# Loading w_q and w_k together in wide rows, and projecting the first 256 tokens chunk by chunk over eight PSUM banks

## The chip, the cores and the metric

The kernel runs on one core of one Trainium2 chip. The metric is the device time of one execution in microseconds (us); lower is better. The engines are named as in the profile: PE (matmul), PEld (its weight loads), DVE, ACT, POOL, and SP, which here only issues DMAs.

## The reference

One transformer block on 2048 tokens of width 448: sliding-window attention (window 256, 16 heads of 28), then a gated MLP whose gate mixes tokens, both with adaptive layer norm. All in bf16.

```python
mod = (silu(c) @ w_mod).reshape(1, 6, 1, 448)        # c is (1, 448)
sa, ca, ga, sb, cb, gb = six rows of mod
h = layernorm(x) * (1 + ca) + sa
q, k, v = h @ wqkv, split into 16 heads of 28
p = softmax(q k^T * 28**-0.5, where 0 <= i - j < 256)
x = x + ga * ((p v) @ wo)
h = layernorm(x) * (1 + cb) + sb
z = gelu_tanh(h @ w_in);  z1, z2 = halves of 896;  z2 = layernorm(z2)
x = x + gb * ((z1 * (w_sp @ z2 + b_sp)) @ w_out)     # w_sp is (2048, 2048)
```

## The kernel before, in words

Tokens lie in 16 tiles of 128 (`x_sb`). The work is written as about 1200 operations, each made by `add` with the engines that may run it, its dependencies and the buffers or PSUM banks (`Hold`) that it takes. A string `ORDER` at the top of the file then says everything about the schedule: each word is `operation.engine`, followed by the number of the bank or buffer taken where there is one (`p` PE, `a` ACT, `v` DVE, `g` POOL, `s` SP). Every engine runs its words strictly in that sequence, SP's DMA issues too; `waits` puts in the semaphore waits that the dependencies need. So an instruction that waits holds everything behind it on its engine.

The start goes as follows. Token tiles 0 and 1 (`x_half` 0) are loaded first. ACT and SP load the first two sixths of `w_mod` (`d_wmAa`, `d_wmAb`, `d_wmAc`), SP then w_q and w_k into `wq_st`. All matrices of 448 rows are cut into contraction chunks kc = 0, 1, 2 (128 rows each) and 3 (64 rows), and loaded in three pieces: kc 2, kc 0 and 1, kc 3. Matmuls with a single column (L485) make the shift and scale `modT` out of `w_mod`. Meanwhile the layer-norm statistics of the tiles run on DVE (L549, L552, L554) with the power on POOL (L557), and the normalised `xn` (L569 on DVE, L573 on ACT) is transposed by PE (L627) two tiles and two chunks at a time; the evacuation `hT` (L634 ACT, L636 DVE) applies scale and shift. The weights are repacked from 28 to 32 columns a head by `pad` (L540 ACT or DVE, L541 POOL in the trace) into `WQK`.

The first 512 tokens are projected in two halves of 256 (`hf` 0 and 1), in eight groups of four heads: g = 0 to 3 are queries, 4 to 7 keys. For `hf` 0 the matmuls (L676) go chunk by chunk in the order kc = 2, 1, 0, 3 (`FIRST`), so that they can begin before all chunks are there; for `hf` 1 a group's four chunks go at once. In the kernel before, the loop runs over queries and keys in turn (`qk`): four groups' banks are held, the chunks of the first two are spread over two pairs of groups, and one chain of dependencies (`done_`) runs through both pairs. Evacuations to `qT` and `KT` are on ACT (L703) or DVE (L704). Matmuls with no use for the result (`warm`, L506) fill PE's time at the start.

Scores (L826) of the first unit need all queries of the first 512 tokens and the keys of the first 256. Exponentials of scores are on ACT (L859, L891), masks on DVE and POOL (L869, L906, L909), P V on PE (L935). The output of attention and the second layer norm's `xn2` are transposed by DMA (`turn`, L429, on SP's queue), which also transposes `w_sp` into `wspA` and `wspB`. Then come the MLP's matmuls: L1014 (z2), L1060 (z1), L1084 (token mixing, groups of 16 matmuls into one of eight banks, each followed by L1088 on DVE, which adds `bsp_bc`, and L1091 on POOL, which multiplies by z1), and L1103 (the output).

Of the kernel before, what the change touches and what calls it, by code (L numbers as in the profile page):

```python
# [4 lines left out]
ACT = mybir.ActivationFunctionType  # L5
# [208 lines left out]
def bass_adaLN_cond__sliding_block__mixer_gmlp__prompt_kernel(  # L214
# [70 lines left out]
    KT, kt_off, kt_bytes = alloc("KT", [128, 4, S], BF16)  # L285
# [12 lines left out]
    qT, _, qt_bytes = alloc("qT", [128, 4, S], BF16, at=wspA_off)  # L298
# [4 lines left out]
    wq_st, _, wq_bytes = alloc("wq_st", [128, DC, 2 * D], BF16, at=z2_off + wmod_bytes)  # L303
# [16 lines left out]
    ps = nc.alloc_psum_tensor("ps", [128, 8, 512], F32)  # L320
# [11 lines left out]
    bA = View(banks, [(6,), (7,), (0,), (1,), (2,), (3,), (4,), (5,)])  # L332
# [23 lines left out]
    def x_load(e, i):  # L356
        return e.dma_start(x_sb[:, 4 * i:4 * i + 4, :], x_d[:, 4 * i:4 * i + 4, :])

    def head(name, eng, t, d, first, n, cols, prio, land, deps=(), least=2.9):

        if n == 64:
            return load(name, eng, 0.1, lambda e: e.dma_start(t[0:64, 3, cols], d[384:448, cols]), deps, prio, land, least)
        return load(name, eng, 0.1, lambda e: e.dma_start(t[:, first:first + n, cols], d[128 * first:128 * (first + n), cols].rearrange("(c p) n -> p c n", p=128)), deps, prio, land, least)

    def x_half(eng, i, prio, land, least):
        return load("d_x0%d" % i, eng, 0.25, lambda e: e.dma_start(x_sb[:, 2 * i:2 * i + 2, :], x_d[:, 2 * i:2 * i + 2, :]), (), prio, land, least)

    t_x0 = [x_half("sp", 0, -98.99, 2.9, 2.9), x_half("sp", 1, -98.935, 7.7, 3.5)]
    t_x = [None]
    ALL = slice(None)  # L370
    LO, HI, BOTH = slice(0, D), slice(D, 2 * D), slice(0, 2 * D)
    t_c = load("d_c", "act", 0.01, lambda e: e.dma_start(c_row[:, 0:D], c[0:1, :]), prio=-98.98, land=1.6, least=1.5)
    t_wmA = [head("d_wmAa", "act", wmod, w_mod, 0, 2, BOTH, -98.97, 5.0, least=4.2), head("d_wmAb", "sp", wmod, w_mod, 2, 1, BOTH, -98.97, 4.1, least=3.4),
             head("d_wmAc", "sp", wmod, w_mod, 3, 64, BOTH, -98.96, 5.5, least=3.8)]
    t_wq = []
    for k, (n, cols, at) in enumerate((("q", LO, (5.8, 6.6, 6.8)), ("k", HI, (8.1, 8.9, 9.1)))):
        a, b, c_ = [head("d_w%s%s" % (n, p), "sp", wq_st, A_wqkv, first, rows, cols, -98.95 + 0.03 * k + 0.004 * i, at[i], (), 3.9)
                    for i, (p, first, rows) in enumerate((("b", 2, 1), ("a", 0, 2), ("c", 3, 64)))]
        t_wq.append([b, b, a, c_])

# [30 lines left out]
    def either(da, fa, dd, fd, deps=(), prio=0.0, take=()):  # L411
        return add({"act": (da, fa), "dve": (dd, fd)}, deps, prio, take)
# [20 lines left out]
    def pe(dur, fns, deps=(), prio=0.0, take=(), shape="full"):  # L433
        op = add({"pe": (dur, fns)}, deps, prio, take, lat=0.2 if shape == "rows32" else PEL)
        op.shape = shape
        return op
# [106 lines left out]
    t_wqk = [[pad(kc, k, -49.5 + 0.2 * k) for kc in range(DC)] for k in range(2)]  # L543
# [40 lines left out]
    QK_ready = {}  # L584
    V_ready = {}
    qkv_ops = {}
    K_ready = {}
# [5 lines left out]
    for tb in range(NB4):  # L593
        v = 40.0 * tb - 50.0
# [12 lines left out]
        ms = []  # L607
# [14 lines left out]
        evh = [[None] * DC, [None] * DC]  # L622
        for hf in range(2 if tb == 0 else 0):
            xl = [xs[2 * hf], xs[2 * hf + 1]]
            for cp, chs in enumerate(((2, 0), (1, 3))):
                h = Hold(bX)
# [4 lines left out]
                for k in range(2):  # L631
                    ch = chs[k]
                    ev = either(
                        0.57, lambda e, h=h, ch=ch, k=k, hf=hf: e.activation(hT[:, ch, hf * 256:(hf + 1) * 256], pst(h, k * 256, (k + 1) * 256), ACT.Identity,  # L634
                                                                            bias=modT[:, ch:ch + 1], scale=modT[:, 4 + ch:5 + ch]),
                        0.41, lambda e, h=h, ch=ch, k=k, hf=hf: e.tensor_scalar(hT[:, ch, hf * 256:(hf + 1) * 256], pst(h, k * 256, (k + 1) * 256),  # L636
                                                                               modT[:, 4 + ch:5 + ch], modT[:, ch:ch + 1], ALU.mult, ALU.add),
                        [m, t_modA] + one_bank, v + 0.5 * hf + cp * 0.1)
# [8 lines left out]
        for cp in range(2 if tb == 1 else 0):  # L647
            h = Hold(bX)
# [9 lines left out]
            for k in range(2):  # L658
                ch = 2 * cp + k
                ev = either(  # L660
                    0.77, lambda e, h=h, ch=ch, k=k, tb=tb: e.activation(hT[:, ch, tb * 512:(tb + 1) * 512], pst(h, k * 512, (k + 1) * 512), ACT.Identity,
                                                                        bias=modT[:, ch:ch + 1], scale=modT[:, 4 + ch:5 + ch]),
                    0.55, lambda e, h=h, ch=ch, k=k, tb=tb: e.tensor_scalar(hT[:, ch, tb * 512:(tb + 1) * 512], pst(h, k * 512, (k + 1) * 512),
                                                                           modT[:, 4 + ch:5 + ch], modT[:, ch:ch + 1], ALU.mult, ALU.add),
                    m + [t_modA] + evs[2 * cp:], v + cp * 0.1)
# [7 lines left out]
        FIRST = (2, 1, 0, 3)  # L673

        def part(g, kc, h, hf):
            return lambda e: e.matmul(ps[:, h.slot[0], 0:256], lhsT=WQK[:, kc, 4 * g:4 * g + 4, :].rearrange("p a b -> p (a b)"),  # L676
                                      rhs=hT[:, kc, hf * 256:(hf + 1) * 256], start=(kc == FIRST[0]), stop=(kc == FIRST[-1]))

        MMH = 256 / 2400.0 + 0.003
        for hf in range(2 if tb == 0 else 0):  # L680
            for qk in range(2):
                four = range(4 * qk, 4 * qk + 4)
                hq = {g: Hold(bA) for g in four}
                last = {}
                vv = v + 1 + 0.5 * hf + 0.2 * qk
                if hf == 0:
                    done_ = []
                    for kc in FIRST[:-1]:
                        for n in range(2):
                            pair = four[2 * n:2 * n + 2]  # L690
                            done_ = [pe(2 * MMH, [part(g, kc, hq[g], hf) for g in pair], [evh[hf][kc], t_wqk[qk][kc], done_], vv + kc * 0.01, [] if kc != FIRST[0] else [hq[g] for g in pair])]
                            ms += done_
                    for g in four:
                        last[g] = pe(MMH, [part(g, FIRST[-1], hq[g], hf)], [evh[hf], t_wqk[qk], done_], vv + 0.03 + 0.001 * g)
                else:
                    for g in four:
                        last[g] = pe(4 * MMH, [part(g, kc, hq[g], hf) for kc in FIRST], [evh[hf], t_wqk[qk]], vv + 0.001 * g, [hq[g]])
                for g in four:
                    h = hq[g]
                    ms.append(last[g])  # L700
                    to = (lambda g=g, hf=hf: qT[:, g, hf * 256:(hf + 1) * 256]) if g < 4 else (lambda g=g, hf=hf: KT[:, g - 4, hf * 256:(hf + 1) * 256])
                    ev = either(
                        0.39, lambda e, h=h, to=to: e.activation(to(), ps[:, h.slot[0], 0:256], ACT.Copy),  # L703
                        0.43, lambda e, h=h, to=to: e.tensor_copy(to(), ps[:, h.slot[0], 0:256]),  # L704
                        [last[g]], vv)
                    h.until.append(ev)
                    if g < 4:
                        QK_ready.setdefault((g, 0), []).append(ev)
                    else:
                        for i in (2 * hf, 2 * hf + 1):  # L710
                            K_ready[(g - 4, i)] = ev
        for k, g in enumerate(range(0 if tb == 0 else 4 if tb in FINE else 8)):
            h = Hold(bX)
# [5 lines left out]
            if g < 4:  # L719
                to = lambda g=g, tb=tb: qT[:, g, tb * 512:(tb + 1) * 512]  # L720
            else:
                to = lambda g=g, tb=tb: KT[:, g - 4, tb * 512:(tb + 1) * 512]
            ev = either(
                0.6, lambda e, h=h, to=to: e.activation(to(), ps[:, h.slot[0], :], ACT.Copy),
                0.68, lambda e, h=h, to=to: e.tensor_copy(to(), ps[:, h.slot[0], :]),
                [m], v + 1 + k * 0.1)
# [6 lines left out]
        for i in range(4):  # L733
            t = 4 * tb + i
            if tb in FINE:
                v = 10.0 * t - 20.0
                h = Hold(bX)
# [4 lines left out]
                ev = either(  # L742
                    0.6, lambda e, h=h, t=t: e.activation(KT[:, :, t * 128:(t + 1) * 128], ps[:, h.slot[0], :].rearrange("p (g n) -> p g n", g=4), ACT.Copy),
                    0.68, lambda e, h=h, t=t: e.tensor_copy(KT[:, :, t * 128:(t + 1) * 128], ps[:, h.slot[0], :].rearrange("p (g n) -> p g n", g=4)),
                    [m], v + 1)
# [442 lines left out]
```

## Time and profile before

| | |
|---|---|
| device time, median of 3 runs | 271.91 us (271.07 to 272.81) |
| the profiled execution | 273.37 us, of which the profile's span is 271.5 us |
| PE busy | 260.9 us (96%), 2897 matmuls |
| PEld busy | 136.2 us (50%) |
| DVE busy | 155.2 us (57%) |
| ACT busy | 131.8 us (49%), nothing after 60% of the span |
| POOL busy | 133.1 us (49%) |
| HBM | 9.53 MB read, 1.84 MB written |

In the profile every line of an answer names a line of the kernel, an engine, an operation and its tiles, with how often it ran (x) and how long. In answers over stretches of time, the first number after the stretch is its length, followed by the busy time and count of each engine, the granted clock of PE (1.00 is full), the share of time that the DMA engines were busy and the GB/s that they moved. The time between an instruction's end and the next one's start is idle time, and the name after an arrow is what ended it. For a DMA the profile gives when it was issued, and the time from there to its landing.

### The profile page before, as it was taken

The page shows a single profiled execution, that of the slowest core. Times are in us where ns is not written, and L with a number is a line of the kernel's source. Part 1 is how long each engine was busy: PE and PEld are TensorE (multiplying, and loading weights), DVE is VectorE, ACT ScalarE, POOL GpSimd, SP SyncE. Part 2 cuts the span into 40 slices and gives each one's busy share as a digit, 9 for nine tenths or more (in the row PEclk, how much of TensorE's full clock was granted, in tenths as well). Part 3 has the DMA queues.
Part 4 walks back from the last instruction along what each step waited for, and adds up shares of the span by engine and source line. Part 5 has one row for each costly group of instructions (what it writes and reads, how often), then busy time and mean ns, then how long its engine had stood idle before and what let it go on. Part 6 is the DMA issues. An engine that isn't in the chain of part 4 may idle for free.

```text
span 271.5 us, 6828 instructions
## 1 busy us (share of the span) xinstructions
PE 260.9 (96%) x2897; PEld 136.2 (50%) x2916; DVE 155.2 (57%) x363; ACT 131.8 (49%) x190; POOL 133.1 (49%) x175
## 2 busy tenths in 40 slices
PE   7899999999999988999999999999999999999996
PEld 2674465556567555444444444444444444445454
DVE  6689998999999998973874000112233201314354
ACT  3589998999999993889896500000000000000000
POOL 5538756557279983856578000043477501633110
PEclk9799999999999999999999999999999999999999
DMA  7991668765273695838999990000000000000222
GB/s 214 269 334 38 141 109 106 136 99 128 56 119 64 114 94 92 205 77 102 191 176 221 170 197 16 0 2 0 0 0 2 0 0 0 2 17 17 85 69 86
DMA packets 66777, 25.45 MB, mean 94 GB/s; under 512 B 57846, under 2 KB 66043, under 8 KB 66747
## 3 DMA queue, kind: packets, MB, share of 16 engines
q1 hardware_dynamic: 66328, 24.52, 47.4%
q8 instruction: 23, 0.38, 0.6%
q10 hardware_dynamic: 418, 0.50, 0.6%
q14 instruction: 8, 0.06, 0.1%
HBM read 9.53 MB, written 1.84 MB: 42 GB/s over the span
## 4 chain that ended last, share of the span: by engine, by line
PE 81%; ACT 7%; DVE 5%; DMA 4%; issue 1%; ACTq 0%; DVEq 0%
PE ps L1084 35%; PE ps L1060 8%; PE ps L1103 8%; PE ps L1014 7%; PE ps L714 6%; PE ps L826 4%; ACT PA L859 4%; PE ps L935 3%; ACT PA L891 3%; PE ps L751 3%; PE ps L676 2%; DMA wmod<-in_w_mod_dram 2%; PE ps L958 2%; DMA hT<-o_sb 2%; DVE PA L906 1%
## 5 line engine op out<-in xcount | busy, mean ns | idle before, releaser
L1091 POOL TENSOR_TENSOR z1T<-tmpg,z1T 128x512 bf16<-128x512 bf16 x28 | 31.9, 1154 | 78.0 <-DVE tmpg L1088 78.0
L1088 DVE TENSOR_TENSOR tmpg<-ps,bsp_bc 128x512 bf16<-128x512 f32 x28 | 19.0, 690 | 81.7 <-PE ps L1084 70.6
L859 ACT ACTIVATE PA<-ps 128x1536 bf16<-128x1536 f32 (+4 forms) x64 | 60.3, 976 | 1.8 <-PE ps L826 1.0
L1084 PE MATMUL ps<-wspA,z 128*128 128x512 bf16 x220 | 49.1, 379 | 0.3 <-issue 0.2
L1084 PE MATMUL ps<-wspB,z 128*128 128x512 bf16 x218 | 49.0, 379 | 0.3
L1084 PEld LDWEIGHTS ps<-wspA,z 128*128 128x128 bf16 x224 | 21.9, 98 | 26.5 <-issue 0.4
L1084 PEld LDWEIGHTS ps<-wspB,z 128*128 128x128 bf16 x224 | 21.9, 98 | 26.4
L557 POOL TENSOR_TENSOR rs_all<-ve_all,neghalf 128x1 f32<-128x1 f32 (+1 forms) x31 | 21.2, 693 | 12.4 <-DVE ve_all L554 10.4
L869 POOL TENSOR_TENSOR PA<-PA,mask 128x1024 bf16<-128x1024 bf16 (+1 forms) x9 | 18.6, 2068 | 11.7 <-ACT PA L859 11.7
L935 PEld LDWEIGHTS ps<-Vaug,PA 128*128 128x128 bf16 x720 | 20.8, 96 | 4.8 <-issue 0.8
L1014 PE MATMUL ps<-w_in,hT 64*128 64x448 bf16 x224 | 22.4, 349 | 0.5 <-DVE PA L906 0.3
L935 PE MATMUL ps<-Vaug,PA 128*128 128x32 bf16 x720 | 22.1, 176 | 0.1
L1103 PE MATMUL ps<-w_out_g,z1T 128*128 128x448 bf16 (+3 forms) x126 | 21.9, 332 | 0.0
L1060 PE MATMUL ps<-hT,w_in 64*128 64x512 bf16 x196 | 21.8, 376 | 0.0
L826 PE MATMUL ps<-qT,KT 32*64 32x64 bf16 (+3 forms) x768 | 18.1, 223 | 2.1 <-ACT PA L859 1.0
L549 DVE BATCH_NORM_STATS2 st_all<-x_sb 128x6 f32<-128x448 bf16 x32 | 19.3, 612 | 0.1
L714 PE MATMUL ps<-hT,WQK 128*128 128x512 bf16 x72 | 17.9, 379 | 0.9 <-issue 0.3
L891 ACT ACTIVATE PA<-ps 128x1536 bf16<-128x1536 f32 (+1 forms) x16 | 16.4, 1024 | 1.6 <-PE ps L826 1.0
L906 DVE TENSOR_TENSOR PA<-PA,mask 128x2048 bf16<-128x2048 bf16 x14 | 17.0, 1212 | 0.2 <-ACT PA L859 0.2
L1114 DVE TENSOR_TENSOR fin<-ps,x_sb 128x448 bf16<-128x448 f32 (+3 forms) x18 | 10.0, 570 | 12.2 <-PE ps L1103 10.9
L1103 PEld LDWEIGHTS ps<-w_out_g,z1T 128*128 128x128 bf16 x126 | 11.8, 98 | 10.0 <-DVE fin L1114 0.2
L1068 ACT ACTIVATE z1T<-ps 128x512 bf16<-128x512 f32 x28 | 14.5, 608 | 3.6 <-PE ps L1060 3.5
(114 smaller groups left out, 334.8 us busy)
## 6 DMA issues: line engine op xcount, KB each, us to landing
w_in<-in_B_w_in_dram SPq DMA_DIRECT2D x8, 224.0 KB, 3.4
out_dram<-fin SPq DMA_DIRECT2D x15, 112.0 KB, 1.7
x_sb<-in_A_x_dram SPq DMA_DIRECT2D x3, 448.0 KB, 6.7
wmod<-in_w_mod_dram SPq DMA_DIRECT2D x1, 1344.0 KB, 10.3
w_out_g<-in_B_w_out_dram SPq DMA_DIRECT2D x1, 784.0 KB, 5.0
bsp_bc<-in_B_b_sp_dram SPq DMA_DIRECT2D x1, 512.0 KB, 4.6
x_sb<-in_A_x_dram SPq DMA_DIRECT2D x2, 224.0 KB, 4.0
wmod<-in_w_mod_dram SPq DMA_DIRECT2D x2, 224.0 KB, 5.6
```

The lines of the kernel that those rows point to most:

```text
L557: rs = pool(0.41 + 0.155 * len(tiles), lambda e: e.tensor_tensor(rs_all[:, slot, a:b], ve_all[:, slot, a:b], neghalf[:, 0:b - a], ALU.pow) ...
L714: m = pe(4 * MMS, [lambda e, h=h, g=g, kc=kc, tb=tb: e.matmul(ps[:, h.slot[0], :], lhsT=WQK[:, kc, 4 * g:4 * g + 4, :].rearrange("p a b -> ...
L826: return [lambda e, t=t: e.matmul(to(t), lhsT=KT[32 * t:32 * t + 32, qi, key:key + kn], rhs=qT[32 * t:32 * t + 32, qi, q0:q0 + qn], start= ...
L859: return e.activation(cols(place(kb, hf) + 64 + 768 * a, [[384, 2 * (b - a)], [1, w]]), ps[:, h.slot[0]:h.slot[0] + b - a, 2 * n * w:(2 * ...
L891: return e.activation(cols(EXTRAS[ext[n].slot[0]] + 128 * a, [[128, b - a], [512, 4], [1, 128]]), ps[:, h.slot[0]:h.slot[0] + b - a, :].re ...
L906: return e.tensor_tensor(cols(a, [[d, 2], [384, 16], [1, 64]]), cols(src(), [[0, 2], [64, 16], [1, 64]]), mask_ap([[64 if m else 192, 2], ...
L935: fns.append(lambda e, hO=hO, hd=hd, bi=bi, kb=kb, nb=nb, j=j, c=(2 * t + k) * 384 + 128 * (j - kb), half=half: e.matmul(ps[:, hO.slot[0], ...
L1014: return lambda e, kc, p0, start, stop: e.matmul(ps[:, hs[t % 2].slot[hf], 0:D], lhsT=hT[p0:p0 + 64, kc, t * 128:(t + 1) * 128], rhs=w_in[ ...
L1060: return lambda e, kc, p0, start, stop: e.matmul(ps[:, hs[b // 2].slot[b % 2], :], lhsT=w_in[p0:p0 + 64, kc, ft * 128:(ft + 1) * 128], rhs ...
L1084: m = pe(16 * MMS, [lambda e, h=h, si=si, ft=ft, tb=tb: e.matmul(ps[:, h.slot[0], :], lhsT=z2[:, si, ft * 128:(ft + 1) * 128], rhs=(wspA i ...
L1091: u = pool(1.16, lambda e, ht=ht, ft=ft, tb=tb: e.tensor_tensor(z1T[tb][:, ft, :], tmpg[:, ht.slot[0], :], z1T[tb][:, ft, :], ALU.mult), [ ...
L1103: return [lambda e, ft=ft: e.matmul(ps[:, h.slot[0], c0:c1], lhsT=z1T[t // 4][:, ft, (t % 4) * 128:(t % 4 + 1) * 128], rhs=w_out_g[:, ft, ...
```

## The change

The six loads of w_q and w_k (three pieces of each, rows of 448 elements) become three loads with rows of 896 elements, and the second pair of token tiles (`x_half` 1) is issued between the first and the second of them instead of between w_q and w_k. The projection of `hf` 0 holds eight banks, one for each group, and goes through its chunks for each pair of groups with a chain of dependencies of its own; `hf` 1's groups are made in one loop of eight.

```diff
-    t_x0 = [x_half("sp", 0, -98.99, 2.9, 2.9), x_half("sp", 1, -98.935, 7.7, 3.5)]
+    t_x0 = [x_half("sp", 0, -98.99, 2.9, 2.9), x_half("sp", 1, -98.94, 6.8, 3.5)]
...
-    t_wq = []
-    for k, (n, cols, at) in enumerate((("q", LO, (5.8, 6.6, 6.8)), ("k", HI, (8.1, 8.9, 9.1)))):
-        a, b, c_ = [head("d_w%s%s" % (n, p), "sp", wq_st, A_wqkv, first, rows, cols, -98.95 + 0.03 * k + 0.004 * i, at[i], (), 3.9)
-                    for i, (p, first, rows) in enumerate((("b", 2, 1), ("a", 0, 2), ("c", 3, 64)))]
-        t_wq.append([b, b, a, c_])
+    wqb, wqa, wqc = [head("d_wqk" + p, "sp", wq_st, A_wqkv, first, rows, BOTH, -98.95 + 0.02 * i, at, (), 3.9)
+                     for i, (p, first, rows, at) in enumerate((("b", 2, 1, 6.05), ("a", 0, 2, 7.9), ("c", 3, 64, 8.2)))]
+    t_wq = [[wqa, wqa, wqb, wqc]] * 2
...
         for hf in range(2 if tb == 0 else 0):
-            for qk in range(2):
-                four = range(4 * qk, 4 * qk + 4)
-                hq = {g: Hold(bA) for g in four}
-                last = {}
-                vv = v + 1 + 0.5 * hf + 0.2 * qk
+            hq = {g: Hold(bA) for g in range(8)}
+            last = {}
+            vv = v + 1 + 0.5 * hf
+            for n in range(4):
+                pair = (2 * n, 2 * n + 1)
+                done_ = []
                 if hf == 0:
-                    done_ = []
                     for kc in FIRST[:-1]:
-                        for n in range(2):
-                            pair = four[2 * n:2 * n + 2]
-                            done_ = [pe(2 * MMH, [part(g, kc, hq[g], hf) for g in pair], [evh[hf][kc], t_wqk[qk][kc], done_], ...)]
-                            ms += done_
-                    for g in four:
-                        last[g] = pe(MMH, [part(g, FIRST[-1], hq[g], hf)], [evh[hf], t_wqk[qk], done_], ...)
+                        done_ = [pe(2 * MMH, [part(g, kc, hq[g], hf) for g in pair], [evh[hf][kc], t_wqk[n // 2][kc], done_], ...)]
+                        ms += done_
+                for g in pair:
+                    if hf == 0:
+                        last[g] = pe(MMH, [part(g, FIRST[-1], hq[g], hf)], [evh[hf], t_wqk[n // 2], done_], ...)
+                    else:
+                        last[g] = pe(4 * MMH, [part(g, kc, hq[g], hf) for kc in FIRST], [evh[hf], t_wqk[n // 2]], ...)
```

The evacuations behind it are the same eight for each half. The whole `ORDER` string is another one. What it changes, read word by word against the one before:

- SP's first issues were: x pair 0, w_mod kc 2, w_mod kc 3, w_q kc 2, w_q kc 0 and 1, w_q kc 3, x pair 1, w_k kc 2, w_k kc 0 and 1, w_k kc 3, x tiles 4 to 7, w_v, w_mod (rest), w_v (last chunk), x tiles 8 to 11, and so on. They become: x pair 0, w_mod kc 2, w_mod kc 3, w_q and w_k kc 2, x pair 1, w_q and w_k kc 0 and 1, w_q and w_k kc 3, x tiles 4 to 7, w_o (last chunk), w_v (last chunk), x tiles 8 to 11, w_v, w_mod (rest), and so on. One transpose of `w_sp` that stood among the first 20 is moved behind the first transposes of attention. The load of `b_sp`, which had stood 12 `w_sp` transposes behind the last `hT` transpose, stands 24 behind it, and w_out is loaded behind that last `hT` transpose too.
- PE runs 16 `warm` matmuls instead of 13. The first transposes, the pairs of groups and the groups change places; when the first scores come, the same 32 matmuls of `hf` 0 and 20 of `hf` 1 stand before them.
- 86 of the operations go to another engine. At the start, the four evacuations of the first transposes are all on ACT (it was one), and the eight `pad` operations are three on DVE, three on POOL and two on ACT (they were five on ACT and three on POOL). DVE does the three of w_q's chunks 1, 0 and 3, among the statistics of token tiles 2 and 3.
- The activation L471, whose result nobody uses and which makes ACT load its table early, moves from the start of ACT's list to behind all but two of the MLP's activations.

More of the change, by code (lines that the diff above doesn't have):

```diff
@@ L688, in bass_adaLN_cond__sliding_block__mixer_gmlp__prompt_kernel @@
                     for kc in FIRST[:-1]:
-                        for n in range(2):
-                            pair = four[2 * n:2 * n + 2]
-                            done_ = [pe(2 * MMH, [part(g, kc, hq[g], hf) for g in pair], [evh[hf][kc], t_wqk[qk][kc], done_], vv + kc * 0.01, [] if kc != FIRST[0] else [hq[g] for g in pair])]
-                            ms += done_
-                    for g in four:
-                        last[g] = pe(MMH, [part(g, FIRST[-1], hq[g], hf)], [evh[hf], t_wqk[qk], done_], vv + 0.03 + 0.001 * g)
-                else:
-                    for g in four:
-                        last[g] = pe(4 * MMH, [part(g, kc, hq[g], hf) for kc in FIRST], [evh[hf], t_wqk[qk]], vv + 0.001 * g, [hq[g]])
@@ L698, in bass_adaLN_cond__sliding_block__mixer_gmlp__prompt_kernel @@
[L698 to L711, printed above, removed]
+                        done_ = [pe(2 * MMH, [part(g, kc, hq[g], hf) for g in pair], [evh[hf][kc], t_wqk[n // 2][kc], done_], vv + kc * 0.01, [] if kc != FIRST[0] else [hq[g] for g in pair])]
@@ new lines, in bass_adaLN_cond__sliding_block__mixer_gmlp__prompt_kernel @@
+                        ms += done_
+                for g in pair:
+                    if hf == 0:
+                        last[g] = pe(MMH, [part(g, FIRST[-1], hq[g], hf)], [evh[hf], t_wqk[n // 2], done_], vv + 0.03 + 0.001 * g)
+                    else:
+                        last[g] = pe(4 * MMH, [part(g, kc, hq[g], hf) for kc in FIRST], [evh[hf], t_wqk[n // 2]], vv + 0.001 * g, [hq[g]])
+            for g in range(8):
+                h = hq[g]
+                ms.append(last[g])
+                to = (lambda g=g, hf=hf: qT[:, g, hf * 256:(hf + 1) * 256]) if g < 4 else (lambda g=g, hf=hf: KT[:, g - 4, hf * 256:(hf + 1) * 256])
+                ev = either(
+                    0.39, lambda e, h=h, to=to: e.activation(to(), ps[:, h.slot[0], 0:256], ACT.Copy),
+                    0.43, lambda e, h=h, to=to: e.tensor_copy(to(), ps[:, h.slot[0], 0:256]),
+                    [last[g]], vv)
+                h.until.append(ev)
+                if g < 4:
+                    QK_ready.setdefault((g, 0), []).append(ev)
+                else:
+                    for i in (2 * hf, 2 * hf + 1):
+                        K_ready[(g - 4, i)] = ev
```

2 lines of the change are left out of this document (1 added, 1 removed).

## The prediction

> **What bounds the kernel now.** I read the engine shares first, then busy time by stretches, then the chain that ended last, then the first 20 us instruction by instruction.
>
> ```profile
> span 271.5 us, 6828 instructions
> ```
> ```profile
> 17.59:50.00 32.41, 31.14 (x553) 16.82 (x560) 30.07 (x68) 30.80 (x36) 22.96 (x21) 1.00 0.69 120
> 50.00:90.00 40.00, 38.86 (x902) 25.17 (x908) 38.45 (x80) 38.50 (x43) 25.05 (x32) 1.00 0.53 96
> 90.00:109.27 19.27, 17.45 (x368) 10.22 (x366) 18.18 (x42) 14.87 (x22) 13.92 (x18) 1.00 0.80 106
> 109.27:151.00 41.73, 41.59 (x400) 19.57 (x402) 27.45 (x89) 35.13 (x66) 27.45 (x52) 1.00 0.90 162
> 151.00:268.70 117.70, 117.21 (x564) 55.38 (x572) 28.01 (x44) 2.94 (x6) 34.81 (x31) 1.00 0.15 34
> ```
>
> The columns after the length are busy us of PE, PEld, DVE, ACT and POOL, then granted clock, DMA share and GB/s. From 109.27 us on PE is busy 99.6% of the time: no order of the same matmuls makes that part shorter. In the attention stage (17.59 to 90) PE, ACT and DVE are all about 95 to 97% busy. PE's gaps from 17.59 to 109.27 are 1.27 + 1.14 + 1.82 = 4.23 us; that is the most that a new order can win there, whatever it does. So the time is the moment at which the first scores (L826) start, plus a fixed amount of matmul work, plus these gaps.
>
> The start itself:
>
> ```profile
> 7.36 0.75 PE L485 MATMUL ps<-sc_sb,wmod 128*128 128x1 bf16 x24 [0.76 <-DMA wmod<-in_w_mod_dram]
> ```
> ```profile
> 9.69 3.61 PE L676 MATMUL ps<-hT,WQK 128*128 128x256 bf16 x22
> 13.54 0.61 PE L627 MATMUL ps<-ident,xn 128*128 128x128 bf16 x8 [0.24 <-ACT qT L703]
> 13.99 3.57 PE L676 MATMUL ps<-hT,WQK 128*128 128x256 bf16 x30
> 17.59 0.70 PE L826 MATMUL ps<-qT,KT 32*64 32x64 bf16 x64
> ```
> ```profile
> 9.86 0.62 DVE L549 BATCH_NORM_STATS2 st_all<-x_sb 128x6 f32<-128x448 bf16 x1
> ```
> ```profile
> 11.93 0.95 DVE L569 TENSOR_SCALAR xn<-x_sb,mv_all,rs_all 128x448 bf16<-128x448 bf16 x2
> ```
>
> The first 22 projection matmuls take 164 ns each, the next 30 take 119 ns: the clock.
>
> ```profile
> 8.00:8.25 0.25, 0.25 (x9) 0.19 (x5) 0.10 (x2) 0.25 (x1) 0.00 (x0) 1.00 1.12 380
> 8.50:8.75 0.25, 0.25 (x4) 0.25 (x5) 0.25 (x1) 0.06 (x2) 0.00 (x0) 0.50 0.56 179
> ```
> ```profile
> 12.00:12.25 0.25, 0.25 (x4) 0.23 (x3) 0.25 (x1) 0.00 (x0) 0.25 (x2) 1.00 1.03 143
> ```
>
> It is halved between about 8.4 and 11.8 us. When the first scores start, both versions have done the same matmuls (32 of the first 256 tokens, 20 of the next 256: four query groups and one key group), so that moment compares them fairly.
>
> **The change, part by part. The loads.**
>
> ```profile
> 2.41 1.05 SPq L363 DMA_DIRECT2D wq_st<-in_A_wqkv_dram  x2
> 3.51 0.48 SPq L362 DMA_DIRECT2D wq_st<-in_A_wqkv_dram  x1
> 4.03 0.59 SPq L366 DMA_DIRECT2D x_sb<-in_A_x_dram  x1
> ```
> ```profile
> wq_st<-in_A_wqkv_dram SPq DMA_DIRECT2D x1, 224.0 KB, 5.7
> ```
> ```profile
> x_sb<-in_A_x_dram SPq DMA_DIRECT2D x1, 224.0 KB, 5.6
> ```
> ```profile
> 7.00:11.00 4.00, 3.34 (x40) 2.46 (x42) 2.67 (x9) 2.70 (x6) 1.58 (x4) 0.68 1.00 297
> 15.00:18.00 3.00, 2.96 (x76) 2.27 (x73) 3.00 (x11) 2.81 (x9) 0.00 (x0) 1.00 1.03 400
> ```
>
> Three issues of about 0.5 us go away on SP; nothing is waiting behind them, since the next load (x tiles 4 to 7) waits for w_mod until 7.7 us anyway. The bytes are the same. The second x pair landed at 4.03 + 5.6 = 9.63; with 224 KB of weights ahead of it instead of 392 KB it comes 168 KB sooner, at 297 GB/s 0.58 us: about 9.05. The query chunks 0 and 1 landed at 2.94 + 5.7 = 8.64 (2.94 is the second issue of the pair at 2.41); now 896 KB end with them instead of 336 KB, 560 KB or 1.93 us more: about 10.6. The last piece comes with the same total, near 11.0. Whether rows of 1792 B move faster than rows of 896 B no row here separates: the bounds are nothing and the 400 GB/s that w_mod's 3584-byte rows reached, which over these 1008 KB would be 0.9 us. I take nothing, because 7 to 11 us, with the 896-byte rows, already kept the engines' share at 1.00. [...]
>
> **The chain to the first scores.** DVE no longer evacuates the first half's transposes (ACT does, four instead of one), so statistics of the second pair can start at 9.05 instead of 9.86. But DVE now holds three weight pads and a memset (0.24 us) ahead of the two normalisations:
>
> ```profile
> L569 DVE TENSOR_SCALAR xn<-x_sb,mv_all,rs_all 128x448 bf16<-128x448 bf16 x16 | 6.6, 415 | 2.5 <-POOL ve_all L564 1.8 <-POOL rs_all L557 0.6
> ```
>
> A pad on DVE has no row: above, the 415 ns of a same-sized DVE instruction; below, half of it. I take 0.3, nearer to the DVE row. Statistics end at 10.4, the first pad stalls DVE to 10.6 (its chunk lands then), and pad, aggregate, pad, variance, pad, shift, memset, two normalisations (0.3+0.2+0.3+0.15+0.3+0.15+0.24+0.8) end at about 13.05; before, 11.93 + 0.95 = 12.88. PE's order puts the second transposes behind the first query groups, so they start near 13.1 to 13.2, before 13.54. After them come 33 projection matmuls before the scores, not 30: 13.2 + 0.6 + 33 x 0.119 = 17.7. ACT may be later than that:
>
> ```profile
> 13.02 0.94 ACT L703 ACTIVATE qT<-ps 128x256 bf16<-128x256 f32 x3 [1.49 <-PE ps L676]
> ```
>
> From about 13.9 it has a pad and an hT quarter (0.56 each) and ten such evacuations (0.31 apart) left: 4.2 us, 18.1. The projection's second half also takes banks that these evacuations free, so PE cannot run ahead. Scores: 17.9, **+0.3 us**; bounds 17.25 (transposes at 13.05 that cost PE 0.25 beside the 33 matmuls, evacuations never late) and 18.3, so -0.35 to +0.7. The three added warm-up matmuls stand where PE waits for hT or pads; without that cover each costs about 0.33 us at half clock (twice the 164 ns of half as many columns).
>
> The activation whose only use is to bring in the table early moves to the end of ACT's list. The load is not late for it:
>
> ```profile
> 102.35 1.28 ACT L1025 ACT_TABLE_LOAD   x1
> 107.70 0.92 ACT L1025 ACTIVATE z<-ps 128x896 bf16<-128x896 f32 x1 [4.06 <-PE ps L935]
> ```
>
> A load ran 4.06 us ahead of the wait of its own activation; for the first Tanh it will run just as early, behind ACT's two DMA issues. Cost nothing.
>
> **The attention stage.** Between the first and the last exponential ACT's list held 14 evacuations (8 of V, 6 of 512-wide q and k) and now holds 13 (6 of V, 5 of q and k, one of 256, the gate).
>
> ```profile
> L755 ACT ACTIVATE Vaug<-ps 128x448 bf16<-128x448 f32 x8 | 4.5, 561 | 0.0
> ```
> ```profile
> L724 ACT ACTIVATE qT<-ps 128x512 bf16<-128x512 f32 x3 | 1.8, 599 | 0.0
> ```
> ```profile
> L869 DVE TENSOR_TENSOR PA<-PA,mask 128x1024 bf16<-128x1024 bf16 x20 | 13.9, 709 | 0.3 <-ACT PA L859 0.3
> ```
> ```profile
> L869 POOL TENSOR_TENSOR PA<-PA,mask 128x1024 bf16<-128x1024 bf16 x8 | 17.4, 2183 | 10.9 <-ACT PA L859 10.9
> ```
>
> ACT: 8 x 0.56 + 6 x 0.6 = 8.1 before, 6 x 0.56 + 5 x 0.6 + 0.4 + 0.58 = 7.3 after: -0.8 us. DVE takes these (two of V and one of q and k, about +1.9) and one mask of 0.71 and a half one of 0.56 from POOL (which is spared 2.18 each), and gives away three normalisations (3 x 0.415), the gate and one 256 evacuation (1.0) and small operations: about +0.2 us on balance, bounds 0 and +1. With all three engines at 95%, the stage gains only what the busiest of them gains: I take **-0.2 us**, bounds -0.8 and +0.2.
>
> **The transition.** SP issues in order. The load of one gate row and that of w_out, each 0.57 us, stood among the transposes at 96 to 107 us; now they come before and after. On the chain there lies one piece,
>
> ```profile
> 97.10 5.45 DMA hT<-o_sb
> ```
>
> The gate row was issued just before it; half of its 0.57 us taken: **-0.3 us**, bounds -0.57 and 0.
>
> **The sum**: +0.3 - 0.2 - 0.3 = -0.2, a span of 271.3. The profiled execution took 273.37 for its span of 271.5, and the median run 271.91; so 271.7 for the median.
>
> **The rivals.** First, *the bias is late*. The load of b_sp stood 12 transposes behind the last hT transpose; now 24 of them and w_out stand there.
>
> ```profile
> 142.91 0.58 SPq L989 DMA_DIRECT2D bsp_bc<-in_B_b_sp_dram  x1
> ```
> ```profile
> 144.74 16.96 SPq L429 DMA_TRANSPOSE wspB<-in_B_w_sp_dram  x11
> ```
> ```profile
> 151.02 17.21 PE L1084 MATMUL ps<-wspA,z 128*128 128x512 bf16 x78 [0.16 <-issue]
> ```
> ```profile
> bsp_bc<-in_B_b_sp_dram SPq DMA_DIRECT2D x1, 512.0 KB, 4.6
> ```
> ```profile
> wmod<-in_w_mod_dram SPq DMA_DIRECT2D x1, 1344.0 KB, 10.3
> ```
> ```profile
> L1091 POOL TENSOR_TENSOR z1T<-tmpg,z1T 128x512 bf16<-128x512 bf16 x28 | 31.9, 1154 | 78.0 <-DVE tmpg L1088 78.0
> L1088 DVE TENSOR_TENSOR tmpg<-ps,bsp_bc 128x512 bf16<-128x512 f32 x28 | 19.0, 690 | 81.7 <-PE ps L1084 70.6
> ```
>
> Twelve more at 1.54 us (11 in 16.96) and 0.57 move its issue to about 162.0, with 4.6 to 166.6. PE's groups of 16 take 3.44 us; the seventh (at 171.7) takes the bank of the fourth, whose addition (L1088) comes as the fourth: two at 0.69, then two that wait for POOL (1.15), done at 170.4. It is hidden with 1.3 us left; from a landing time of 5.9 us it decides, and at w_mod's 10.3 us PE stands for 4.4: 276.3. The margin speaks against it, the small size of the margin for it. 0.09.
>
> Second, *the second x pair was never the gate*: DVE was busy to 9.95, and the pads use up what is won; the rest of the order gains nothing. Head +0.3, remainder 0: 272.2. The landing at 9.63 speaks for it. 0.18.
>
> Third, *the clock stays down*: the queries now wait for chunks that land at 10.6, so PE may do too little before 11.8 and the half clock last as long again, 3.4 us at 164 instead of 119 ns: 3.4 x (1 - 119/164) = 0.9, with the head's 0.3 a time of 273.1. Against it, warm-ups and pair work fill PE there. 0.09. [...]
>
> Fourth, *the order closes the gaps*: two thirds of the 4.23 us (2.8) and the head's -0.35: 268.8. For it, ACT is relieved; against it, PE and DVE are not. 0.07.
>
> **How the numbers follow.** Forecast 271.7: 0.53, own range 270.7 to 272.6. Rivals 0.09, 0.18, 0.09, 0.07; 0.04 for a stall of another kind beyond 3 us. A measurement here can tell about 1% (2.7 us) from no change. Faster by more: the fourth rival, 0.07. Slower by more: the first and the rest, 0.13. Within: 0.80. The range 269.8 to 274.0 takes in the third case and the bounds of the head and the stage, and leaves out 0.07 below and most of 0.13 above.
>
> **What would show it.** The second pair's statistics start near 9.1 us; its transposes near 13.2; scores near 17.9; the span from there to 109 us has some 4 us of PE gaps; bsp_bc is issued near 162 and L1088 never holds a bank that PE waits for. A first score before 17.2 or after 18.6, PE gaps under 2 us, or a PE gap near 172 would each show a step wrong.

## The result: 0.9% slower, and the profile after

| | before | changed |
|---|---|---|
| median of 20 runs each | 272.22 us | 274.67 us |
| changed / before, 95% interval | | 1.0088 (1.0063 to 1.0112) |
| profiled execution, its span | 273.37, 271.5 us | 272.92, 271.2 us |

The forecast was 271.7 us, "within 1%", with a range up to 274.0. The time lies above that range. The two profiled executions mislead here: that of before lies 1.15 us above its median, that of the changed kernel 1.75 us below its own.

The stretches of the first profile of the changed kernel, with the columns as in the prediction:

```profile
17.59:50.00 32.41, 29.82 (x510) 16.27 (x514) 31.78 (x63) 30.05 (x37) 22.74 (x20) 1.00 0.39 77
50.00:90.00 40.00, 37.30 (x835) 24.56 (x838) 38.11 (x74) 35.42 (x37) 27.07 (x33) 0.96 0.79 118
90.00:109.27 19.27, 18.75 (x407) 11.82 (x406) 19.06 (x41) 16.18 (x23) 15.75 (x23) 1.00 0.53 91
109.27:151.00 41.73, 41.57 (x403) 19.67 (x399) 26.89 (x92) 35.77 (x66) 25.24 (x48) 1.00 0.84 151
151.00:268.70 117.70, 117.17 (x563) 55.18 (x572) 27.72 (x45) 2.91 (x7) 36.70 (x33) 1.00 0.19 41
```

PE's gaps in the attention stage (first two rows) grew from 2.41 to 5.29 us, those of the transition (third row) shrank from 1.82 to 0.52, and behind 109.27 us nothing changed. The head, in the same execution:

```profile
11.36 0.62 PE L625 MATMUL ps<-ident,xn 128*128 128x128 bf16 x8
...
15.62 0.71 PE L822 MATMUL ps<-qT,KT 32*64 32x64 bf16 x64
```

The first scores came at 15.62 us instead of 17.59. So between these two executions 2 us were won and then lost. Who PE waited for from 15 to 110 us says where (the summary of waits; total, times, longest):

```profile
PE ps L931 <- DVE qT L721: 1.5, 1, 1.5
PE ps L511 <- DVE hT L661: 1.5, 1, 1.5
```

Two single stalls, both behind DVE. What DVE and POOL did before each of them (timeline; start, length):

```profile
20.50 0.66 DVE L905 TENSOR_TENSOR PA<-PA,mask 128x1024 bf16<-128x1024 bf16 x1
20.82 2.31 POOL L865 TENSOR_TENSOR PA<-PA,mask 128x1024 bf16<-128x1024 bf16 x1 [0.49 <-ACT PA L855]
21.08 2.14 DVE L478 COPY sc_rep<-sc_sb 128x128 bf16<-128x128 bf16 x1
23.14 2.14 DVE L661 TENSOR_SCALAR hT<-ps,modT 128x512 bf16<-128x512 bf16 x4
24.31 0.94 PE L511 MATMUL ps<-wmod,sc_rep 128*32 128x448 bf16 x16 [1.50 <-DVE hT L661]
...
73.25 2.13 POOL L865 TENSOR_TENSOR PA<-PA,mask 128x1024 bf16<-128x1024 bf16 x1 [1.26 <-ACT PA L855]
73.32 3.15 DVE L902 TENSOR_TENSOR PA<-PA,mask 128x2048 bf16<-128x2048 bf16 x1
75.47 1.08 POOL L552 TENSOR_SCALAR ve_all<-mv_all 128x1 f32<-128x1 f32 x1
...
77.13 0.46 PE L931 MATMUL ps<-Vaug,PA 128*128 128x32 bf16 x12 [1.53 <-DVE qT L721]
```

The same copy before, and the masks of 128x2048 before and changed (groups of instructions; busy us, mean ns):

```profile
16.12 0.21 DVE L480 COPY sc_rep<-sc_sb 128x128 bf16<-128x128 bf16 x1
...
L906 DVE TENSOR_TENSOR PA<-PA,mask 128x2048 bf16<-128x2048 bf16 x14 | 17.0, 1212 | 0.2 <-ACT PA L859 0.2
...
L902 DVE TENSOR_TENSOR PA<-PA,mask 128x2048 bf16<-128x2048 bf16 x14 | 19.1, 1373 | 0.1
```

The copy to `sc_rep`, an operand of the gate's matmuls (L511), has 128x128 elements; it "takes" 2.14 us and ends with POOL's mask, at 23.1 us. A mask of 128x2048 takes 3.15 us where the other thirteen take about 1.2; it started 0.07 us after POOL's mask, and POOL's next small instruction (L552) then took 1.08 us, where its median is 0.23, until DVE's mask was done. No wait is shown: the profile books the standing as busy time of DVE. That is part of why DVE reads 98% busy in the first row above. A third stall of the same kind, in the head, is in the second profile of this kernel (two normalisations in 2.10 us, e10 below) and not in this one (0.94 us).

After the second stall the clock fell, too. One window of 0.25 us before, one inside and one behind (the column after POOL's is the granted clock):

```profile
77.75:78.00 0.25, 0.25 (x9) 0.25 (x7) 0.25 (x2) 0.00 (x0) 0.00 (x0) 1.00 0.75 147
...
78.25:78.50 0.25, 0.25 (x5) 0.25 (x3) 0.25 (x3) 0.00 (x0) 0.08 (x1) 0.50 1.73 514
...
81.50:81.75 0.25, 0.25 (x12) 0.25 (x11) 0.02 (x1) 0.25 (x1) 0.25 (x1) 1.00 0.00 0
```

It was halved from about 78.0 to 81.4 us (the windows of 0.25 us from 78.00 and from 81.25 read 0.53 and 0.64). Such a stretch lowers the mean clock of an execution by 0.006; of the 20 runs of the changed kernel five had a mean of 1.0, nine of 0.994 and six of 0.988, with medians of about 273.6, 274.6 and 276.2 us.

### The profile page after: what moved, and what is told of

It reads as the page before. It is cut to its first block, busy times and chain, and to the rows that moved or that the text cites. A ratio compares the mean times of both kernels' runs of the same rounds, so it can differ in the third digit from the quotient of the medians.

```text
span 271.2 us, 6834 instructions
## 1 busy us (share of the span) xinstructions
PE 260.6 (96%) x2898; PEld 137.3 (51%) x2919; DVE 157.4 (58%) x358; ACT 131.3 (48%) x189; POOL 138.2 (51%) x181
## 4 chain that ended last, share of the span: by engine, by line
PE 76%; ACT 10%; DVE 8%; POOL 4%; issue 1%; ACTq 0%
PE ps L1080 35%; PE ps L1099 8%; PE ps L1010 7%; ACT PA L855 5%; PE ps L710 4%; PE ps L822 4%; PE ps L931 3%; PE ps L747 3%; PE ps L954 3%; ACT PA L887 3%; PE ps L1056 3%; PE ps L674 2%; PE ps L504 2%; PE ps L734 1%; POOL rs_all L555 1%
## 5 line engine op out<-in xcount | busy, mean ns | idle before, releaser
L931 PEld LDWEIGHTS ps<-Vaug,PA 128*128 128x128 bf16 x720 | 21.0, 96 | 7.0 <-DVE qT L721 1.8
L931 PE MATMUL ps<-Vaug,PA 128*128 128x32 bf16 x720 | 22.6, 177 | 1.5 <-DVE qT L721 1.5
L555 POOL TENSOR_TENSOR rs_all<-ve_all,neghalf 128x1 f32<-128x1 f32 (+1 forms) x31 | 20.1, 655 | 6.5 <-DVE ve_all L552 6.1
L865 POOL TENSOR_TENSOR PA<-PA,mask 128x1024 bf16<-128x1024 bf16 x7 | 16.8, 2396 | 7.6 <-ACT PA L855 7.6
L902 DVE TENSOR_TENSOR PA<-PA,mask 128x2048 bf16<-128x2048 bf16 x14 | 19.1, 1373 | 0.1
L574 POOL TENSOR_SCALAR xn<-x_sb,rs_all,ve_all 128x448 bf16<-128x448 bf16 x18 | 16.9, 944 | 3.7 <-DVE ve_all L559 2.7
L865 DVE TENSOR_TENSOR PA<-PA,mask 128x1024 bf16<-128x1024 bf16 (+1 forms) x25 | 16.3, 667 | 0.0
```

What stands on the lines that cost most here:

```text
L555: rs = pool(0.41 + 0.155 * len(tiles), lambda e: e.tensor_tensor(rs_all[:, slot, a:b], ve_all[:, slot, a:b], neghalf[:, 0:b - a], ALU.pow) ...
L865: mk = lambda e, hf=hf, tri=tri: e.tensor_tensor(cols(place(kb, hf) + 64, [[384, 8], [192, tri], [1, 64]]), cols(place(kb, hf) + 64, [[384 ...
L931: fns.append(lambda e, hO=hO, hd=hd, bi=bi, kb=kb, nb=nb, j=j, c=(2 * t + k) * 384 + 128 * (j - kb), half=half: e.matmul(ps[:, hO.slot[0], ...
```

## The experiments

**Theory A**: some instructions of DVE and POOL shut each other out, as the copy (2.14 us, 0.21 before) and the mask (3.15 us, 1.2 before) suggest; the changed order lets DVE come second in a few places, and PE stands. **Theory B**: the new order is slower in many small waits, and a stall that is removed only moves on. **Theory C**: the head's gain is none that lasts.

In the table, "rest" is the profiled span less the start of the first scores in the same profile. The kernel before ran beside each group, with medians of 271.81 (e1 to e4), 272.53 (e5 to e8) and 271.61 us (e9 to e11), so the ratios are what compares. They are worked out over the single runs and need not be the plain quotient of two medians.

| | median | against before (95%) | first scores | rest |
|---|---|---|---|---|
| before, first profile | 272.22 | 1 | 17.59 | 253.9 |
| e8 before, second profile | 271.49 (one run) | | 16.09 | 253.6 |
| changed, first profile | 274.67 | 1.0088 (1.0063 to 1.0112) | 15.62 | 255.6 |
| e10 changed, second profile | 274.28 (one run) | | 17.07 | 255.5 |
| e1 copy early | 271.89 | 1.0008 (0.9990 to 1.0026) | 16.57 | 253.6 |
| e11 mask on DVE | 272.10 | 1.0015 (0.9988 to 1.0041) | 17.02 | 255.3 |
| e5 POOL waits at 10 us | 272.51 | 1.0002 (0.9975 to 1.0029) | 15.63 | 254.6 |
| e2 copy early, mask on DVE | 269.33 | 0.9919 (0.9889 to 0.9949) | 15.54 | 251.8 |
| e6 all three | 269.52 | 0.9885 (0.9851 to 0.9919) | 16.56 | 251.5 |
| e3 changed head, order of before behind | 274.85 | 1.0093 (1.0061 to 1.0124) | 17.29 | 254.7 |
| e4 before with the wide loads | 272.79 | 1.0030 (1.0013 to 1.0047) | 16.85 | 253.7 |
| e7 before, copy planted at 22.8 us | 272.31 | 0.9983 (0.9959 to 1.0007) | 17.49 | 253.3 |
| e9 before, copy planted later | 273.51 | 1.0063 (1.0043 to 1.0083) | 16.75 | 255.3 |

**e1, the copy early.** One word of the order moves:

```diff
-... 203.p.0 208.v ... 206.p.5 53.v 240.v ...
+... 203.p.0 53.v 208.v ... 206.p.5 240.v ...
```

> The changed kernel with one word moved: DVE's copy to sc_rep stands before the evacuation at 14.75 us, when POOL is idle, instead of at 21.08 us beside POOL's mask, where it took 2.14 us. Theory A (DVE and POOL shut each other out; two such stalls on DVE, of the copy at 21 us and of a mask of 128x2048 at 73 us with 3.15 us, give the head's gain back): the copy takes about 0.2 us, hT is there 1.9 us earlier, PE's 1.5 us of idle time before the gate's matmuls goes, and the median falls by about 1.5, from 274.7 to 273.2 (272.7 to 273.8). Theory B (the new order of the rest is slower in many small waits, and a stall that is taken away only moves the wait on): the median stays within 0.5 of 274.7.

The stall of L511 is gone and that of L931 is left. Measured against the kernel before, the 0.9% is gone. That is more than A expected (271.89 us, below 272.7); its stretches of halved clock became rare as well (2 of 12 runs, 15 of 20 before this edit). B is out. The profile showed something new in the head:

```profile
10.02 2.23 DVE L567 TENSOR_SCALAR xn<-x_sb,mv_all,rs_all 128x448 bf16<-128x448 bf16 x2
...
9.94 0.23 POOL L465 COPY mask<-mask 128x64 bf16<-128x64 bf16 x1
10.12 0.55 POOL L539 COPY WQK<-wq_st 128x448 bf16<-128x448 bf16 x1
10.62 1.21 POOL L455 MEMSET Vaug<- 128x256 bf16 x1
...
12.31 0.62 PE L625 MATMUL ps<-ident,xn 128*128 128x128 bf16 x8 [1.53 <-DVE xn L567]
```

The two normalisations that gate the head took 2.23 us, not 0.94: here POOL's copy, pad and memset came first. This is the race at 10 us below.

**e2, also one mask from POOL to DVE.**

```diff
-... 467.g 468.v ...
+... 467.v 468.v ...
```

> As e1, and one mask of 128x1024 that POOL ran at 73.25 us runs on DVE instead (about 0.68 us there), so that DVE's mask of 128x2048 behind it has nothing to stand still for. Theory A: that mask takes 1.2 us instead of 3.15, PE's idle 1.5 us at 75.6 goes and with it the half clock from 78.1 to 81.35 that cost about 1.6 us; the median is about 271.0 (270.0 to 272.2), below the kernel before. Theory B: 274 or more.

Below A's range (269.33 against 270.0 to 272.2), and none of the six runs had a stretch of halved clock. The mask of 128x2048 takes its usual time again,

```profile
71.14 1.29 DVE L865 TENSOR_TENSOR PA<-PA,mask 128x1024 bf16<-128x1024 bf16 x2 [0.15 <-ACT PA L855]
72.35 1.22 DVE L902 TENSOR_TENSOR PA<-PA,mask 128x2048 bf16<-128x2048 bf16 x1
```

and PE's wait behind it is 0.20 us. This kernel beats both the changed one and the one before, with one word moved and one changed.

**e11, the mask alone.** Only the second of these two edits.

> The changed kernel with the one mask of 128x1024 on DVE instead of POOL, and nothing else (the copy to sc_rep stays where it stands still). Theory A: from e1 to e2 this edit was worth 2.6 us, so the median falls from 274.7 to about 272.2 (271.6 to 272.8). If the two stalls hide each other, less: 273.5 or more.

272.10, as A expected. Of the two later stalls its profile keeps the copy's, and in that execution the clock was down behind that one: its mean from 17.59 to 50 us was 0.95 (1.00 in e10), and the 16 matmuls of L511 took 1.53 us (0.94 in e10).

**e5 and e6, POOL waits at 10 us.**

```diff
+        if tb == 0:
+            for late_ in (t_va[1], t_wqk[1][0]):
+                late_.deps.update((xs[2], xs[3]))
```

> The changed kernel, in which POOL's pad of one key chunk (10.5 us) and its memset of the ones column (1.2 us) wait until DVE's two normalisations of the second x pair (10.36 to 11.30) are done; everything else as changed. Theory A (DVE and POOL shut each other out, and who comes first at 10.4 us differs from run to run: in the profile of the changed kernel DVE came first and PE did not wait, in e1 and e3 POOL came first, DVE's pair took 2.23 us instead of 0.94 and PE stood 1.53 us): every run is now like the profiled one, the median falls from 274.7 to about 273.0 (272.6 to 273.6) and the spread narrows to about 1.5 us. Theory B (the profiled run was merely lucky in its transfers): 274.2 to 274.9, with the spread as it was.

> e2 (the copy to sc_rep early, one mask moved to DVE) and e5 (POOL waits for the two normalisations) together. Theory A: as e2's faster runs, 268.9 (268.5 to 269.4), with no run above 270. Theory B: no better than e2, 269.3 or more, with runs up to 270.8.

e5 won a little more than expected (272.51, just below A's range). Its profile has both later stalls but no halved clock; its spread did not narrow as A had it (271.43 to 274.74), and six of its twelve runs still had such a stretch. The median of e6, 269.52, lies above A's range (268.5 to 269.4), where B had it, and is no lower than e2's. No run of e6 was above 269.83, while e2 had two of its six at 270.8; with six runs each, that the race sets the spread of e2 is likely but not shown. Against the kernel before, e6 and e2 are the fastest kernels here, by 1.2 and 0.8%, with intervals that overlap.

In e6's profile the normalisations ran without a stall and the first scores were late all the same:

```profile
11.54 0.70 DVE L567 TENSOR_SCALAR xn<-x_sb,mv_all,rs_all 128x448 bf16<-128x448 bf16 x2
...
16.56 0.70 PE L825 MATMUL ps<-qT,KT 32*64 32x64 bf16 x64
```

DVE's first pad, which waits for the load of its weights, started at 10.29 us there and at 9.36 in e5: the loads do not land at the same time in each execution.

**e8 and e10, second profiles of the two kernels.**

> The kernel before once more, for a second profile. Its first profile, with 273.37 us, lies above its median and shows the clock halved from 8.4 to 11.8 us. If that stretch is usual, the first scores start at 17.6 us again; if it is not, they start about 0.8 us earlier (22 matmuls at 119 instead of 164 ns would be 1.0 us), and as much of the 2 us by which the changed kernel's head looked faster is not the change's.

> The changed kernel once more, for a profile of a usual run: its first profile, with 272.92 us, is 1.75 under its median. Theory A: about 274.5, with the pair of normalisations at 10 us at 2.2 us instead of 0.94 (POOL's pad and memset come first), the first scores near 16.6 to 17 us instead of 15.62, the stalls of the copy (about 2.1 us) and of the mask of 128x2048 (about 3.1 us) as in the first profile. Theory B: none of the three differs from the first profile, and the 1.6 us lie elsewhere.

```profile
12.02 0.62 PE L627 MATMUL ps<-ident,xn 128*128 128x128 bf16 x8 [0.95 <-DVE xn L569]
...
16.09 0.71 PE L826 MATMUL ps<-qT,KT 32*64 32x64 bf16 x64
```

This is before (e8): no halved clock in the head, and the first scores 1.5 us sooner than in its first profile. Not all of that is the clock's: the 24 matmuls of `w_mod` started at 6.55 us instead of 7.36, ahead of the halved stretch. The changed kernel in a usual run (e10):

```profile
10.66 2.10 DVE L567 TENSOR_SCALAR xn<-x_sb,mv_all,rs_all 128x448 bf16<-128x448 bf16 x2
...
11.12 1.21 POOL L455 MEMSET Vaug<- 128x256 bf16 x1
...
17.07 0.71 PE L822 MATMUL ps<-qT,KT 32*64 32x64 bf16 x64
...
22.53 2.15 DVE L478 COPY sc_rep<-sc_sb 128x128 bf16<-128x128 bf16 x1
...
74.74 3.14 DVE L902 TENSOR_TENSOR PA<-PA,mask 128x2048 bf16<-128x2048 bf16 x1
```

All three stalls, as A expected. Between these two executions the head is 1.0 us slower, not 2 us faster, and the rest 1.9 us slower: 2.9 of span, where the medians differ by 2.45. Each is one execution, and e8 lies 1.0 us below the median of its group.

**e7 and e9, the stall planted in the kernel before.** The copy (word 56.v) moves into POOL's pair of masks, ahead of 243.v (e7) or 217.v (e9).

> The kernel before with one word moved the other way: DVE's copy to sc_rep leaves its place at 16.1 us (0.21 us) and stands ahead of the first scaling of hT for tokens 512 to 1023, at about 23.0 us, while POOL runs its two masks from 22.88 to 27.09. Theory A: the copy stands until POOL's mask ends, 2 us or more instead of 0.2, the four scalings of hT behind it come that much later, and the median rises by 1.5 to 2.5 us. Theory B (the copy is slow for another reason, or DVE has slack there): under 0.4 us.

> As e7, where the copy to sc_rep started 0.02 us after POOL's mask and still took 0.20 us while POOL's pair of masks took 4.29 instead of 4.21 us: DVE had come first. Here the copy stands one scaling of hT further back, about 0.5 us into POOL's first mask. [...] Theory B: 0.2 us, no change in the median.

e7 missed: its copy was recorded 0.02 us after POOL's mask and was not held up, and POOL's pair took 4.29 us (4.20 in e9).

```profile
22.79 0.20 DVE L480 COPY sc_rep<-sc_sb 128x128 bf16<-128x128 bf16 x1
...
22.77 4.29 POOL L869 TENSOR_TENSOR PA<-PA,mask 128x1024 bf16<-128x1024 bf16 x2 [1.32 <-ACT PA L859]
...
25.34 0.59 DVE L549 BATCH_NORM_STATS2 st_all<-x_sb 128x6 f32<-128x448 bf16 x1
```

e9 hit. The copy, which started 0.6 us into POOL's first mask, took 1.60 us, until about the middle of POOL's pair, and the median rose by 1.9 us, within what A had given for e7 (1.5 to 2.5):

```profile
22.80 1.60 DVE L480 COPY sc_rep<-sc_sb 128x128 bf16<-128x128 bf16 x1
24.32 0.41 DVE L704 CAST KT<-ps 128x256 bf16<-128x256 f32 x1
24.74 1.54 DVE L663 TENSOR_SCALAR hT<-ps,modT 128x512 bf16<-128x512 bf16 x3
...
22.20 4.20 POOL L869 TENSOR_TENSOR PA<-PA,mask 128x1024 bf16<-128x1024 bf16 x2 [1.41 <-ACT PA L859]
...
24.79 0.40 PE L826 MATMUL ps<-qT,KT 32*128 32x256 bf16 x8 [1.28 <-DVE KT L704]
```

This is the same copy, on the same data, in the kernel that was the faster one. The rows below it matter as much: beside POOL's second mask, DVE's evacuations out of PSUM ran at their usual length (L704 0.41 us, in the mean before 0.415; three of L663 in 1.54, 0.53 each before), and so did the statistics in e7 (0.59 us at 25.34, 0.61 before). Of the forms in these rows only the copy stood.

**e3 and e4, parts of the change.** e3 takes the changed order up to word 203.p.0, the last ahead of the first scores, and from there the words of before with their engines. e4 is before with the three wide loads and x pair 1 behind the first of them.

> The changed kernel's loads, projection and order up to the last matmul ahead of the first scores; from there every operation on the engine and in the order of the kernel before. Theory A (the head is worth 2 us and the order of the rest gives it back): first scores at about 15.6 us, the rest as long as before (253.9 us), a span near 269.5 and a median near 270.3 (269.6 to 271.2). Theory C (the head's gain is none that lasts, the attention stage is bound by engines that do not start earlier): 271.8 to 272.6, as the kernel before.

> The kernel before with the wide loads and the second x pair between them alone; projection, banks and order as before. By the prediction the wide rows win nothing and the second pair comes 0.6 us sooner but is no gate: 272.2, within 0.6. If the loads are what made the head faster (w_mod's matmuls started 0.6 us sooner in the changed kernel and the clock was never halved there), the first scores start about 1 us earlier than 17.59 and the median is near 271.2.

e3 missed A's number by 4.5 us. In its profile DVE lost the race at 10 us (2.24 us), and the old order, now at other moments, meets POOL in places where it did not before (one such mask took 0.71 us in the mean before; beside the one at 47.78 us POOL ran L531 from 47.22 us, for 1.54 us):

```profile
39.84 2.81 DVE L865 TENSOR_TENSOR PA<-PA,mask 128x1024 bf16<-128x1024 bf16 x2
...
47.78 1.53 DVE L865 TENSOR_TENSOR PA<-PA,mask 128x1024 bf16<-128x1024 bf16 x1
...
39.19 2.91 POOL L531 TENSOR_TENSOR wo_g<-wo_g,gg_sb 128x448 bf16<-128x448 bf16 x2 [0.51 <-DMA gg_sb<-mod_rows]
```

So it decides nothing on theory C; the 253.6 us of the old rest hold for the old meeting points. What each of these places cost was not separated. e4 says that the loads alone are a loss in the old projection:

```profile
9.81 2.19 PE L674 MATMUL ps<-hT,WQK 128*128 128x256 bf16 x18 [1.06 <-ACT WQK L538]
...
16.85 0.70 PE L824 MATMUL ps<-qT,KT 32*64 32x64 bf16 x64
```

The first pads wait for the wide pieces and PE waits for the pads; the first scores come 0.76 us later than in e8, and the median, the firmer sign, is 1.0 us up.

## Why the prediction was wrong, step by step

**The step that failed** is the attention stage: "DVE takes these ... about +0.2 us on balance". It added instructions by their mean durations, each engine by itself, and asked which engine's sum grows. It never asked which DVE instruction stands beside which POOL instruction, and of `sc_rep`, whose copy the new order moves from 16.1 us, where POOL was idle, to POOL's first mask, it said nothing. Its sum has a loose end too: the terms that it names come to about +0.9 on DVE, and the small operations that are to bring this to +0.2 have no figure. But what failed is the question, not that size. The stage was to come out at -0.2 (bounds -0.8 to +0.2); PE's gaps there grew by 2.9.

The price by the runs, from single profiles and good to some tenths: without the two stalls the rest is 251.5 to 251.8 us (e6, e2), with both and a full clock 254.6 (e5). So they cost about 3 us, as much as PE stood, twice 1.5. How this splits between copy and mask the profiles do not show: e1, with the mask's stall alone, has 253.6, but in it PE also stood 0.7 us at 66.2 us, which e5 and e6 do not have. By the ratios, taking away the copy's stall alone is worth 0.8% (e1), the mask's alone 0.7% (e11), both 1.7% (e2), so the two add up. These shares include the halved clock. One stretch of it costs 0.9 us by profiles (e10 less e5), and 1.0, 1.2 and 1.7 us by the medians of runs with one and with none (changed, e5, e11). The profile of e11 does not fit the smallest of these: with the copy's stall and one stretch its rest is 255.3. Why the clock cost more there stays open.

Which instructions stood is read from the traces: 2.14 us for a copy of 0.21 (e9: 1.60), 3.15 for a mask of 1.2, 2.23 for a pair of normalisations (e1) that takes 0.70 when POOL waits (e6); a cast out of PSUM took its usual 0.41 beside one of POOL's masks (e9). Why these stood and that did not was not shown.

**The head**: +0.3 expected, 17.9 us. What the change does to it is not shown, because it varies more than that. With the head of before the first scores came at 16.09 (e8), 16.75 (e9), 17.49 (e7) and 17.59 us, with that of the changed kernel at 15.62 and 17.07. The race at 10 us is one reason: PE stood 1.1 to 1.5 us for the normalisations where POOL came first (e10, e1, e11) and 0.2 where DVE did (e2). The loads are another: e7, at full clock, began the 24 matmuls of `w_mod` only at 7.98 us, after a wait for their load, e8 at 6.55; and e6 started late with the race won. The pads on DVE took 0.24 to 0.28 us (0.3 expected). Statistics of the second pair started at 7.70 us, not 9.05: the second pair landed earlier than worked out. That the wide loads win nothing by themselves stands, as e4 has it; e4 does not separate the width of the rows from the order of the pieces.

**The transition**: -0.3 expected, bounds -0.57 and 0; PE's gaps there fell by 1.3 us (1.82 to 0.52). The mechanism, fewer issues between SP's transposes, was not tested by itself; the term was too small.

**The rivals.** The late bias is out: its load was issued at 162.22 us (162.0 was worked out), PE's row behind 151 us is unchanged. "The order closes gaps", 268.8 with a chance of 0.07, is what remains once the stalls are gone: e2 and e6 lie at 269.3 and 269.5, with a rest 2 us shorter than before; which part of the new order wins these 2 us was not tested. "The clock stays down" was right as a price (0.9 us worked out, 0.9 to 1.7 measured) and wrong in place: it came behind the new stalls, not behind the head. In the first profile of the changed kernel the clock fell behind the second stall of 1.5 us (77.1 us) and not behind the first (24.3 us), and in e5, whose PE stood for the same two 1.5 us, it stayed at 1.00 throughout; what decides this was not shown. The forecast of "no change" saw neither the 2 us of better order nor the 4 to 5 us of stalls with the halved clock behind them. That it missed by only 1% is luck: two effects that its sum did not have cancel in part.

## What to carry to other kernels

When an order or an engine is changed, list the pairs that run at the same time on DVE and POOL, and not only the sums: here a DVE copy of 0.2 us that started 0.26 us behind a POOL instruction of 2.31 us took 2.14. An instruction that is far longer than its like of the same shape (3.15 us against 1.2), with no wait shown, is the sign; move it, or give POOL's instruction to DVE or a wait of its own. And take a second profile before building on a first: here two profiles of one kernel had the head 1.5 us apart, for the kernel before and for the changed one, and the first pair made a slower kernel's head look 2 us faster.

## What was not expected of the hardware

- Who came first was a matter of less than 0.1 us: in e7 a copy recorded 0.02 us behind POOL's mask was not held up, in the changed kernel a mask 0.07 us behind took 1.94 us longer than its like. DVE won the race at 10 us in one profile of the changed kernel (0.94 us) and lost it in the other (2.10 us, e10).
- A DVE instruction that stood did not always get its turn when the next POOL instruction ended: in e1 the first of the two normalisations took 1.93 us, beside three POOL instructions in a row (9.94 to 11.83 us), while in e9 the copy got in between two masks.
- After 1.5 us without a matmul the clock was halved in three executions: in the changed kernel's first profile and in e10 behind the second stall, for 3.4 us each, as in the head of before's first profile (8.4 to 11.8 us), and in e11 behind the copy's (a mean of 0.95 from 17.59 to 50 us). After the same 1.5 us it stayed at 1.00 behind both stalls of e5, behind the first of the changed kernel and of e10, and in the head of e1 and e11 (1.53 and 1.54 us).
